# Layer 2 of a three stage kernel: one activation function, seven products of halves for y in four groups, and two sums kept in PSUM

## The chip, the cores and the metric

One core of a Trainium2 chip runs the whole program. The metric is the device time of one execution in microseconds. A kernel is timed several times and the median is given. Beside that, one execution is recorded by the profiler; all rows in this document come from such an execution, and their times count from the start of its span.

## The reference

Three stages follow each other: a linear attention over 4 x 8 heads, whose output is a matrix x of 2304 tokens by 512, and then two dense layers that both widen 512 to 2048 and narrow again.

```python
def _moe_ref(x, w_in, w_out):             # layer 1
    h = x @ w_in
    g = h - np.tanh(h)
    return (g @ w_out).astype(np.float32)

def _moe2_ref(x, w_in, w_out):            # layer 2
    h = x @ w_in
    g = h * (1.0 / (1.0 + np.exp(-1.702 * h)))
    return (g @ w_out).astype(np.float32)
```

The change is in layer 2 and in the work that prepares it.

## The kernel before

**Arithmetic.** Every float32 operand of a dense product is held as two tiles, a rounded high half and the rest as a low half, and a product is three passes of TensorE (`PASSES`: high by high, high by low, low by high). The helper `two(hi, lo, src)` makes them: ScalarE copies `src` to the high half (L423), GpSimd subtracts it for the low half (L424). Weights arrive as 64 bit words and are converted on the way: `cast1` on ScalarE (L284, L286), `cast2a` and `cast2b` on VectorE (L290, L295).

**Layer 1** (`steps`) runs over blocks of 512 tokens; each step makes h for one slice of the 2048 (`h_mm`, L344, twelve matmuls), applies the activation on ScalarE, VectorE and GpSimd (`elem1`, L364 to L374), splits g (L356, L358) and, three steps later (`LAG`), adds the slice's part to y (`y_mm`, L382, twelve matmuls into the PSUM banks y0 to y3). At a block's end `evac` moves y out through VectorE (L403), and the next block's y can start only then.

**Preparing layer 2's weights.** They are needed as sums of quarter blocks, in high and low halves. `conv_ticks` makes them pair by pair (a pair is two slices of 128; `NPAIR` is 8): pieces 0 and 1 of a pair are w_in, pieces 2 and 3 are w_out. The work is cut into ticks "a", "b", "s", "c", "h", "d", "o", "e", which the loops of layer 1 (`L1_TICKS`, one group of ticks per step, pairs 0 to 2) and of layer 2 (`L2_TICKS`, pairs 3 to 7) emit between their own instructions. Pieces go to DRAM (`wfi`, `wfo`) and are loaded again when they are used. In layer 1 the pieces 1 and 3 share the tile `raw2`, and the split pieces wait in `stg` for their stores.

**Layer 2** runs over 24 groups (`GROUPS`): a group n is a pair j of slices for a superblock sb of 768 tokens, taken as 2 x 2 blocks of 384 tokens. Groups 0 to 15 alternate between superblocks 0 and 1; groups 16 to 23 are the third superblock, with pairs 7 down to 0. For h a group needs seven products of block sums instead of eight (`SLOTS`, names P1 to P7; `h_prod`, L813, six matmuls of 384 columns each), one in each of its seven slots. They gather in three PSUM banks a, b and c; `keep` copies a partial sum out (L866), `h_add` adds it to a later one (L862), which gives the four blocks G11, G12, G21 and G22 of h. The activation is a sigmoid on ScalarE (`sig`, L874) and a product on VectorE (`mul`, L877); `gsplit` makes the two halves (L883 on ScalarE, L884 on GpSimd). For y the group has eight chunks (`y_chunk`, L834, six matmuls of 384 columns each) into four PSUM banks `hs`, each added to `yacc` by VectorE (L844). The chunks of group n are emitted in the slots of group n + 1 and the first of n + 2 (`YS`).

**Order.** The program is scheduled by hand: each engine runs its instructions in the order in which the loop emits them. All loads and stores go through SyncE's queue; a store is kept in `later` and emitted at the next `flush`. x for a superblock is split in ticks (`xticks`), one per slot. SBUF pools are stacks: a pool opened in the place of a closed one waits, tile by tile, for the last user of what lay there. The pool `l2left` holds, in order of first use, `win`, `ssum`, `yacc`, `wout`, the seven x tiles of superblock 1, `sp`, `hx`, `sg`, `s7`, `s2` and the tiles of g; below it lay layer 1's x, its elementwise tiles with `ghi` and `glo`, and its late weights.

## Time and profile before

| | |
|---|---|
| Time, median of 3 runs | 918.24 us (916.91 to 918.79) |
| The profiled execution | 917.95 us, span 916.1 us |
| TensorE busy | 900.0 us, 98% of the span, 5192 matmuls |
| VectorE, ScalarE, GpSimd busy | 71%, 61%, 50% |
| Granted TensorE clock, mean | 0.998 of full speed |
| HBM read and written | 98.98 MB, 40.89 MB |

A row of the timeline gives the start in us, the time the instructions took, the engine, the line of the kernel, what was written from what, and how many instructions it merges; square brackets hold the idle time ahead of it and what ended it. PE is TensorE, PEld its weight loads, DVE VectorE, ACT ScalarE, POOL GpSimd, SP SyncE. Consecutive matmuls overlap, so the distance between two starts says more than a duration.

### The profile page before, as it was taken

How to read it: one execution, taken by the hardware profiler on the slowest of the kernel's cores; microseconds unless marked ns; L12 is line 12 of the kernel's file. 1: busy time of each engine (PE TensorE's matmuls, PEld its weight loads, DVE VectorE, ACT ScalarE, POOL GpSimd, SP SyncE). 2: the span in 40 equal slices, each digit the busy share in tenths (PEclk: the TensorE clock that was granted, in tenths of full speed). 3: DMA queues.
4: the chain of work that ended last, by engine and by line, in shares of the span. 5: the costliest groups of instructions: out<-in, count | busy, mean ns of one | idle time of the engine just before them, and what ended most of it. 6: DMA issues, size and time to landing. Idle time of an engine off the chain costs nothing.

```text
span 916.1 us, 14382 instructions
## 1 busy us (share of the span) xinstructions
PE 900.0 (98%) x5192; PEld 819.5 (89%) x5192; DVE 646.4 (71%) x1041; ACT 562.4 (61%) x1175; POOL 462.2 (50%) x361
## 2 busy tenths in 40 slices
PE   8999998999999999998999999999999999999998
PEld 6888887888889888887899889999999999999998
DVE  5899978756766665876867567588888888544454
ACT  5888878776777776767676644345555555433231
POOL 3555534556665665666766544244545564423222
PEclk9999999999999999999999999999999999999999
DMA  6788865131444421585572471224533211444532
GB/s 203 233 260 248 253 228 159 36 138 59 150 138 139 146 103 50 176 287 192 185 268 78 182 274 50 102 98 170 173 130 124 81 56 60 141 160 164 215 147 95
DMA packets 53224, 140.82 MB, mean 154 GB/s; under 512 B 6048, under 2 KB 12832, under 8 KB 50848
## 3 DMA queue, kind: packets, MB, share of 16 engines
q1 hardware_dynamic: 53008, 139.56, 45.0%
q8 instruction: 41, 0.67, 0.3%
q10 hardware_dynamic: 144, 0.33, 0.1%
q14 instruction: 31, 0.25, 0.1%
HBM read 98.98 MB, written 40.89 MB: 153 GB/s over the span
## 4 chain that ended last, share of the span: by engine, by line
PE 87%; DVE 4%; ACT 2%; DMA 2%; POOL 2%; issue 2%; ACTq 0%; POOLq 0%; DVEq 0%
PE hs L834 22%; PE y L382 19%; PE hs L344 18%; PE y L813 18%; PE y L201 3%; DMA raw<-w 2%; PE y L184 2%; PE y L125 1%; PE hs L153 1%; POOL mq L135 1%; DVE pq L139 1%; POOL stg L424 1%; PE hs L813 1%; PE y L228 1%; PE y L180 1%
## 5 line engine op out<-in xcount | busy, mean ns | idle before, releaser
L834 PE MATMUL hs<-g,wout 128*128 128x384 f32 x1152 | 225.4, 334 | 0.0
L344 PE MATMUL hs<-xb,w 128*128 128x512 f32 (+1 forms) x960 | 211.1, 370 | 1.5 <-DVE t L373 1.5
L834 PEld LDWEIGHTS hs<-g,wout 128*128 128x128 f32 x1152 | 202.0, 188 | 0.1
L344 PEld LDWEIGHTS hs<-xb,w 128*128 128x128 f32 x960 | 168.6, 190 | 32.2 <-DVE t L373 1.7
L382 PE MATMUL y<-ghi,w 128*128 128x512 f32 (+1 forms) x640 | 192.4, 368 | 3.2 <-DVE ye L403 3.2
L813 PE MATMUL y<-x,win 128*128 128x384 f32 x966 | 194.0, 335 | 1.3 <-DVE hx L862 1.2
L884 POOL TENSOR_TENSOR g<-sg,g 128x384 fp32r<-128x384 f32 x96 | 103.1, 1074 | 164.7 <-ACT g L883 164.5
L813 PEld LDWEIGHTS y<-x,win 128*128 128x128 f32 x966 | 169.4, 188 | 3.4 <-DVE hx L862 3.4
L358 POOL TENSOR_TENSOR glo<-wq,ghi 128x512 fp32r<-128x512 f32 x72 | 98.2, 1363 | 137.3 <-ACT ghi L356 137.3
L374 DVE COPY_PREDICATED wq<-m,t 128x512 f32<-128x512 uint16 x72 | 83.1, 1155 | 107.4 <-POOL wq L372 107.2
L844 DVE TENSOR_TENSOR yacc<-hs,yacc 128x384 f32<-128x384 f32 x168 | 92.1, 553 | 82.1 <-PE hs L834 81.7
L382 PEld LDWEIGHTS y<-ghi,w 128*128 128x128 f32 x640 | 116.6, 189 | 23.7 <-ACT ghi L356 3.6
L382 PE MATMUL y<-glo,w 128*128 128x512 f32 (+1 forms) x320 | 117.8, 368 | 0.0
L883 ACT CAST g<-sg 128x384 fp32r<-128x384 f32 x96 | 49.5, 515 | 93.8 <-DVE sg L877 93.8
L372 POOL TENSOR_TENSOR wq<-wq,s 128x512 f32<-128x512 f32 x70 | 90.5, 1293 | 20.0 <-DVE wq L371 20.0
L874 ACT ACTIVATE sg<-hx 128x384 f32<-128x384 f32 x72 | 37.9, 526 | 98.8 <-DVE hx L862 97.6
L135 POOL PARTITION_ALL_REDUCE mq<-pq x32 | 65.9, 2107 | 61.5 <-ACT pq L133 61.5
L364 ACT ACTIVATE s<-hs 128x512 f32<-128x512 f32 x72 | 42.9, 596 | 59.6 <-PE hs L344 59.5
L382 PEld LDWEIGHTS y<-glo,w 128*128 128x128 f32 x320 | 60.3, 189 | 9.9
L295 DVE SCALAR_TENSOR_TENSOR raw<-raw 128x512 int32<-128x512 int32 x57 | 61.8, 1084 | 1.6
L371 DVE SCALAR_TENSOR_TENSOR wq<-wq,hs 128x512 f32<-128x512 f32 x72 | 49.0, 681 | 15.7 <-ACT t L366 15.7
L356 ACT CAST ghi<-wq 128x512 fp32r<-128x512 f32 x72 | 44.2, 614 | 22.5 <-DVE wq L374 22.5
(116 smaller groups left out, 1285.4 us busy)
## 6 DMA issues: line engine op xcount, KB each, us to landing
raw<-w SPq DMA_DIRECT2D x57, 512.0 KB, 4.6
xb<-xs SPq DMA_DIRECT2D x24, 512.0 KB, 6.2
win<-wfi SPq DMA_DIRECT2D x9, 1280.0 KB, 8.4
wout<-wfo SPq DMA_DIRECT2D x9, 1024.0 KB, 4.8
vt<-v SPq DMA_DIRECT2D x16, 325.0 KB, 3.5
kt<-kT SPq DMA_DIRECT2D x15, 320.0 KB, 3.4
qt<-qT SPq DMA_DIRECT2D x16, 288.0 KB, 3.5
wfi<-stg SPq DMA_DIRECT2D x9, 512.0 KB, 4.2
```

Source lines behind the costliest of these rows:

```text
L135: nc.gpsimd.partition_all_reduce(mqs[i, j], pq[:, j, :], channels=128, reduce_op=bass.bass_isa.ReduceOp.max)
L295: nc.vector.scalar_tensor_tensor(out=c, in0=c, scalar=3, in1=z, op0=ALU.logical_shift_left, op1=ALU.bitwise_or)
L344: nc.tensor.matmul(h[:, j * n:j * n + n], w[:, 0, a, kt * 128:kt * 128 + 128], x[:, c, kt, :n], start=(k == 0), stop=(k == 11))
L358: nc.gpsimd.tensor_tensor(out=lo, in0=g, in1=hi.bitcast(F32), op=ALU.subtract)
L372: (nc.vector if si < 2 else nc.gpsimd).tensor_tensor(out=w, in0=w, in1=s, op=ALU.mult)
L374: nc.vector.copy_predicated(out=w, mask=m.bitcast(mybir.dt.uint16), data=t)
L382: nc.tensor.matmul(y[d][:, :n], w[:, 1, a, d * 128:d * 128 + 128], g[c][:, j * n:j * n + n], start=(first and j == 0 and k == 0), stop=(la ...
L813: nc.tensor.matmul(dst, w[:, WID[name], a, kt * 128:kt * 128 + 128], xt[:, kt, c, :], start=(first and k == 0), stop=(k == 5), skip_group_ ...
L834: nc.tensor.matmul(dst, wout[j][:, f, a, d * 128:d * 128 + 128], gt[n, f, t][:, c, :], start=(k == 0), stop=(k == 5))
L844: nc.vector.tensor_tensor(out=u, in0=dst, in1=u, op=ALU.add)
L883: nc.scalar.copy(out=u[:, 0, :], in_=g)
L884: nc.gpsimd.tensor_tensor(out=u[:, 1, :], in0=g, in1=u[:, 0, :].bitcast(F32), op=ALU.subtract)
```

## The change

- The activation becomes one ScalarE function (`Gelu_apprx_sigmoid`); `mul` goes. The preload of the table before layer 2 is changed with it.
- `h_add` for G11 (from group 1 on) and for G21 writes its sum back into a PSUM bank, where the activation reads it; `hx` has two tiles.
- In groups 17 to 20 y is formed from seven products of halves (`y_prod`, `y_add`) in place of eight chunks. They need four differences of g blocks (`forms`, `tform`, `tsplit`) on GpSimd, with splits of their own, and four sums of w_out blocks. A product fills two banks, so the four `hs` banks are closed for these groups and opened again after them.
- The sums of w_out for the pairs 3 to 6 are made in new ticks "f", "g" and "i" (`sums2`, `chs`), stored to `wfs`, and loaded by `load_wos`; the next pair's pieces 2 and 3 are loaded after those stores.
- Three low halves per pair go from GpSimd to VectorE in layer 2; in layer 1 `raw2` has two tiles, `stg` six, and the loads are issued earlier; the pool `x0` is opened after the preparation closes; the x tiles of superblock 1 get a pool of their own, `x1`, whose place `yb` takes from group 16 on; `load_win` goes ahead of `load_wout`; one x tick is moved by a slot.

```diff
+L2_STICKS = {2: "f", 3: "g", 6: "i"}
...
+YG, YE = 2 * NPAIR + 1, 3 * NPAIR - NPRE
+YP = ("P3", "P1", "P2", "P6", "P7", "P5", "P4")
...
+    hbanks, banks = ExitStack(), ExitStack()
...
+    psh = pool("psumh", hbanks, space=bass.MemoryType.PSUM)
...
+    wfs = dp.tile([NPAIR, 128, 4 * 512], F32, name="wfs")
...
     def pt(tag):
-        return ps.tile([128, 512], F32, tag=tag, name=tag, bufs=4 if tag == "hs" else 1)
+        return (psh if tag == "hs" else ps).tile([128, 512], F32, tag=tag, name=tag, bufs=4 if tag == "hs" else 1)
...
-            nc.scalar.activation(out=ob, in_=qb, func=AF.Sigmoid)
+            nc.scalar.activation(out=ob, in_=qb, func=AF.Gelu_apprx_sigmoid)
...
-    def two(hi, lo, src, eng=None):
+    def two(hi, lo, src, eng):
...
-        (eng or nc.gpsimd).tensor_tensor(out=lo, in0=src, in1=hi.bitcast(F32), op=ALU.subtract)
+        eng.tensor_tensor(out=lo, in0=src, in1=hi.bitcast(F32), op=ALU.subtract)
...
         def load(q, k):
...
-                t = raw[q, k] = o.tile([128, 512, 2], I32, tag=tag, name="raw2", bufs=1 if tag == "raw2" else 2)
+                t = raw[q, k] = o.tile([128, 512, 2], I32, tag=tag, name="raw2", bufs=2)
...
+        def sums2(q):
+            s = st[q] = p.tile([128, 4, 256], F32, tag="ssum", name="ssum", bufs=1)
+            f1, f2 = f32(q, 2), f32(q, 3)
+            a11, a21, a12, a22 = f1[:, :256], f1[:, 256:], f2[:, :256], f2[:, 256:]
+            for o, x, y, op in (
+                    (s[:, 0, :], a21, a22, ALU.add), (s[:, 2, :], a11, a21, ALU.subtract),
+                    (s[:, 1, :], s[:, 0, :], a11, ALU.subtract), (s[:, 3, :], a12, s[:, 1, :], ALU.subtract)):
+                nc.gpsimd.tensor_tensor(out=o, in0=x, in1=y, op=op)
+        def chs(q, i):
+            t = raw[q, 2 + i // 2].rearrange("p a b -> p (a b)").bitcast(F32R)
+            v = t.rearrange("p (a h c) -> p a h c", h=2, c=256)
+            two(v[:, :, 0, :], v[:, :, 1, :], st[q][:, i:i + 2, :], nc.gpsimd)
+            store(wfs[q, :, i * 512:(i + 2) * 512].rearrange("p (a h c) -> p a h c", h=2, c=256), v.bitcast(F32))
+            later.append((now[0], lambda: load(q + 1, 2 + i // 2)))
         def ch(q, src, i, n):
...
-                t = p.tile([128, 2 * 512], F32R, tag="stg", name="stg", bufs=3)[:, :512 * n]
+                t = p.tile([128, 2 * 512], F32R, tag="stg", name="stg", bufs=6)[:, :512 * n]
...
-            two(v[:, :, 0, :], v[:, :, 1, :], src.rearrange("p (a c) -> p a c", c=256))
+            two(v[:, :, 0, :], v[:, :, 1, :], src.rearrange("p (a c) -> p a c", c=256),
+                nc.vector if place and i == 2 else nc.gpsimd)
...
-                v = p.tile([128, 2 * 512], F32R, tag="stg", name="stg", bufs=3)
+                v = p.tile([128, 2 * 512], F32R, tag="stg", name="stg", bufs=6)
...
-            two(v[:, 0, :], v[:, 1, :], f32(q, k))
+            two(v[:, 0, :], v[:, 1, :], f32(q, k), nc.vector if place else nc.gpsimd)
...
             def last22():
...
-                load(*((q + 1, 1) if place else (q, 3)))
+                load(q + 1, 1)
...
             def out(k):
...
-                load(q + 1, k if place or k == 2 else 1)
+                if not place or q == NPAIR - 1:
+                    load(q + 1, k)
...
         def begin():
-            for k in range(4 if place else 3):
+            for k in range(4):
...
-        return begin, [(x, f) for q in pairs for x, f in pieces(q).items()]
+        extra = [(x, f) for q in pairs if q < NPAIR - 1 for x, f in dict(
+            f=lambda q=q: sums2(q), g=lambda q=q: chs(q, 0), i=lambda q=q: chs(q, 2)).items()]
+        return begin, [(x, f) for q in pairs for x, f in pieces(q).items()], extra
...
-    ticks, xticks = deque(), deque()
+    ticks, sticks, xticks = deque(), deque(), deque()
...
-            xpool[0] = pool("x0", side="right", reuse_waits="tile")
-            for i in range(7):
-                new_x2(0, i)
...
-            begin, ts = conv_ticks(rp, range(NPRE))
+            begin, ts, _ = conv_ticks(rp, range(NPRE))
...
-                for x in L1_TICKS[(sp - LAG - 1) % len(L1_TICKS)]:
+                at = sp - LAG - 1
+                for x in L1_TICKS[at % len(L1_TICKS)]:
...
+                xpool[0] = pool("x0", side="right", reuse_waits="tile")
+                for i in range(7):
+                    new_x2(0, i)
...
+    wos = {}
+    def load_wos(j):
+        wos[j] = yb.tile([128, 4, 2, 256], F32R, tag="wos", name="wos", bufs=2)
+        nc.sync.dma_start(
+            out=wos[j].bitcast(F32), in_=wfs[j].rearrange("p (a h c) -> p a h c", h=2, c=256))
+    ybank, begun = {}, set()
+    def y_prod(n, name):
+        sb, j = GROUPS[n]
+        i = "c" if name in ("P2", "P7", "P4") else "a"
+        if name in ("P1", "P2", "P7"):
+            ybank[n, i] = psb.tile([128, 2, 512], F32, tag="ya" if (i == "a") == (n % 2 == 0) else "yc", name="yb", bufs=1)
+        dst = ybank[n, i]
+        w = dict(P1=lambda a: wout[j][:, 0, a, :256], P2=lambda a: wout[j][:, 1, a, :256],
+                 P4=lambda a: wout[j][:, 1, a, 256:], P5=lambda a: wos[j][:, 0, a], P6=lambda a: wos[j][:, 1, a],
+                 P7=lambda a: wos[j][:, 2, a], P3=lambda a: wos[j][:, 3, a])[name]
+        g = gf[n, dict(P1="B11", P2="B21", P3="B22", P4="T4", P5="T1", P6="T2", P7="T3")[name]]
+        for d in range(2):
+            for k, (a, c) in enumerate(PASSES):
+                nc.tensor.matmul(
+                    dst[:, d, :TW], w(a)[:, d * 128:d * 128 + 128], g[:, c, :],
+                    start=(name in ("P1", "P2", "P7") and k == 0), stop=(k == 2), skip_group_check=True)
+    def y_add(n, name):
+        sb, j = GROUPS[n]
+        src = ybank[n, "c" if name in ("P2", "P7", "P4") else "a"][:, :, :TW]
+        h, t = dict(P1=(0, 0), P2=(0, 0), P3=(0, 1), P4=(1, 0), P5=(1, 1), P6=(1, 0), P7=(1, 1))[name]
+        u = yacc[sb, t, h]
+        nc.vector.tensor_tensor(out=u, in0=src, in1=u, op=ALU.add)
...
-    def h_add(n, i, x, y):
-        t = hx[n, i] = tt("hx", 3)
+    def h_add(n, i, x, y, t=None):
+        t = hx[n, i] = tt("hx", 2) if t is None else t
...
-    def sig(n, i):
-        t = sg[n, i] = tt("sg", 4)
-        nc.scalar.activation(out=t, in_=hx[n, i], func=AF.Sigmoid, scale=1.702)
-    def mul(n, i):
-        nc.vector.tensor_tensor(out=sg[n, i], in0=hx.pop((n, i)), in1=sg[n, i], op=ALU.mult)
+    def act(n, i):
+        if yform(n) and i in (G21, G12):
+            t = sg[n, i] = yb.tile([128, TW], F32, tag="sgb", name="sgb", bufs=3)
+        else:
+            t = sg[n, i] = tt("sg", 4)
+        nc.scalar.activation(out=t, in_=hx.pop((n, i)), func=AF.Gelu_apprx_sigmoid)
+    gf = {}
...
     def gsplit(n, i):
...
-        u = gt[n, f, t] = l2.tile([128, 2, TW], F32R, tag=f"g{f}{t}", name=f"g{f}{t}", bufs=1 if f != t else 2)
-        g = sg.pop((n, i))
+        u = l2.tile([128, 2, TW], F32R, tag=f"g{f}{t}", name=f"g{f}{t}", bufs=1 if f != t else 2)
+        if not yform(n):
+            gt[n, f, t] = u
+        else:
+            gf[n, f"B{f + 1}{t + 1}"] = u
+        g = sg[n, i]
...
+    def tform(n, i, x, y):
+        t = sg[n, i] = yb.tile([128, TW], F32, tag=i, name=i, bufs=1)
+        nc.gpsimd.tensor_tensor(out=t, in0=sg[n, x], in1=sg[n, y], op=ALU.subtract)
+    def tsplit(n, i):
+        u = gf[n, i] = yb.tile([128, 2, TW], F32R, tag=f"f{i}", name=f"f{i}", bufs=1)
+        nc.scalar.copy(out=u[:, 0, :], in_=sg[n, i])
+        nc.gpsimd.tensor_tensor(out=u[:, 1, :], in0=sg[n, i], in1=u[:, 0, :].bitcast(F32), op=ALU.subtract)
...
+    def forms(n, s):
+        if s == 0:
+            tform(n, "T1", G12, G11)
+        elif s == 1:
+            tform(n, "T2", G22, "T1")
+            tsplit(n, "T2")
+        elif s == 2:
+            tform(n, "T3", G22, G12)
+            tsplit(n, "T3")
+        elif s == 3:
+            tsplit(n, "T1")
+        elif s == 4:
+            tform(n, "T4", G21, "T2")
+            tsplit(n, "T4")
+        elif s == 5:
+            gsplit(n, G22)
+    def yform(n):
+        return YG <= n < YE
...
     def vec(n, s):
...
-                h_add(n, G11, a, sv.pop((n, "sp")))
-            if n:
-                mul(n - 1, G12)
+                h_add(n, G11, a, sv.pop((n, "sp")), bank[n, "b"][:, :TW] if n else None)
+            if n and not yform(n - 1):
...
-                sig(n, G11)
+                act(n, G11)
...
-            if n:
+            if n and not yform(n - 1):
...
-                mul(n, G11)
...
-                h_add(n, G21, c, sv.pop((n, "s2")))
+                h_add(n, G21, c, sv.pop((n, "s2")), c)
...
-                sig(n, G21)
+                act(n, G21)
...
-                mul(n, G21)
-                sig(n, G22)
+                act(n, G22)
...
-                mul(n, G22)
...
-                sig(n, G12)
+                act(n, G12)
+        if yform(n - 1):
+            forms(n - 1, s)
...
-    l2 = wpool[1] = xpool[1] = pool("l2left", reuse_waits="tile")
+    l2 = wpool[1] = pool("l2left", reuse_waits="tile")
+    x1 = ExitStack()
+    xpool[1] = pool("x1", x1, reuse_waits="tile")
...
+            if n == 2 * NPAIR and s == 0:
+                x1.close()
+                yb = pool("yb", reuse_waits="tile")
...
-                if n >= m:
+                if n >= m and not yform(n - m):
...
+            m = n - 1 if s else n - 2
+            if m == YG and s == 1:
+                hbanks.close()
+                psb = pool("psumb", banks, space=bass.MemoryType.PSUM, reuse_waits="tile")
+            if yform(m):
+                y_prod(m, YP[s])
...
+            if yform(m):
+                y_add(m, YP[s])
+                if m == YE - 1 and s == 0:
+                    banks.close()
+                    psh = pool("psumh2", space=bass.MemoryType.PSUM, reuse_waits="tile")
...
+            if s == 0 and n > 2:
+                if n == 3:
+                    load_win(2)
+                elif sb == 0 and j < NPAIR - 1:
+                    new_w(j + 1)
+                elif sb == 2 and 0 < j < NPAIR - 1:
+                    load_win(j - 1)
...
-            if s == 0 and n > 2:
-                if n == 3:
-                    load_win(2)
-                elif sb == 0 and j < NPAIR - 1:
-                    new_w(j + 1)
-                elif sb == 2 and 0 < j < NPAIR - 1:
-                    load_win(j - 1)
+            if s == 0 and yform(n):
+                load_wos(j)
...
-                if 3 <= q < 98 or q > 100:
+                if 3 <= q < 98 and q != 6 or q > 100:
...
-                begin, ts = conv_ticks(l2, range(NPRE, NPAIR), place)
+                begin, ts, ss = conv_ticks(l2, range(NPRE, NPAIR), place)
...
-            if ticks:
-                at = q - 7 * (2 * NPRE - 2)
+                sticks.extend(ss)
+            at = q - 7 * (2 * NPRE - 2)
+            if ticks and at >= 0:
...
-                    if at >= 0 and ticks[0][0] == x:
+                    if ticks[0][0] == x:
...
+            if sticks and at >= 14 and at // 7 % 2 == 0 and s in L2_STICKS:
+                assert sticks[0][0] == L2_STICKS[s]
+                sticks.popleft()[1]()
...
-                assert not ticks
+                assert not ticks and not sticks
```

## Rows read from the trace of the kernel before

**Rows 1.** busy time by stretch: length, then busy us of each engine, clock, DMA

```profile
420.00:440.00 20.00, 16.80 (x75) 13.62 (x74) 14.16 (x20) 13.05 (x23) 12.54 (x10) 1.00 0.64 213
440.00:540.00 100.00, 100.00 (x539) 87.48 (x538) 63.39 (x87) 63.23 (x114) 59.35 (x48) 1.00 0.52 183
...
560.00:900.00 340.00, 340.00 (x1956) 338.52 (x1955) 234.77 (x404) 153.64 (x325) 141.74 (x127) 1.00 0.34 124
```

**Rows 2.** timeline at 430 us: start, us, engine, line, tiles, idle before

```profile
429.00 2.88 PE L344 MATMUL hs<-xb,w 128*128 128x512 f32 x12
...
430.67 0.67 ACT L284 ACTIVATE raw<-raw 128x512 f32<-128x512 f32 x1 [2.91 <-DMA raw<-w]
...
432.63 1.70 DVE L295 SCALAR_TENSOR_TENSOR raw<-raw 128x512 int32<-128x512 int32 x1
...
434.26 2.47 DVE L403 TENSOR_TENSOR ye<-y,ye 128x512 f32<-128x512 f32 x4
...
435.08 0.47 PE L382 MATMUL y<-ghi,w 128*128 128x512 f32 x1 [3.20 <-DVE ye L403]
```

**Rows 3.** chain of waits in the same stretch: start, us, what

```profile
420.12 3.08 POOL stg L424 x2
423.22 7.43 DMA raw<-w
```

**Rows 4.** DMA issues: tiles, queue, count, size, us to landing

```profile
raw<-w SPq DMA_DIRECT2D x57, 512.0 KB, 4.6
...
wfi<-win SPq DMA_DIRECT2D x9, 512.0 KB, 2.6
...
wfo<-wout SPq DMA_DIRECT2D x6, 512.0 KB, 6.0
```

**Rows 5.** timeline of TensorE in the third block

```profile
841.40 1.20 PE L813 MATMUL y<-x,win 128*128 128x384 f32 x6
...
842.44 1.20 PE L834 MATMUL hs<-g,wout 128*128 128x384 f32 x6
```

**Rows 6.** lines by shape: count, busy us, mean ns, idle before

```profile
L844 DVE TENSOR_TENSOR yacc<-hs,yacc 128x384 f32<-128x384 f32 x168 | 92.1, 553 | 82.1 <-PE hs L834 81.7
...
L883 ACT CAST g<-sg 128x384 fp32r<-128x384 f32 x96 | 49.5, 515 | 93.8 <-DVE sg L877 93.8
L373 DVE TENSOR_TENSOR t<-hs,t 128x512 f32<-128x512 f32 x72 | 49.1, 682 | 0.0
...
L877 DVE TENSOR_TENSOR sg<-hx,sg 128x384 f32<-128x384 f32 x72 | 47.8, 664 | 0.0
...
L874 ACT ACTIVATE sg<-hx 128x384 f32<-128x384 f32 x72 | 37.9, 526 | 98.8 <-DVE hx L862 97.6 <-POOL x L424 1.2
...
L424 POOL TENSOR_TENSOR win<-raw,win 128x256 fp32r<-128x256 f32 x5 | 3.7, 744 | 4.7 <-ACT win L423 4.7
```

**Rows 7.** timeline of GpSimd and VectorE in the third block

```profile
833.89 1.01 POOL L884 TENSOR_TENSOR g<-sg,g 128x384 fp32r<-128x384 f32 x1 [2.30 <-ACT g L883]
834.32 0.56 DVE L844 TENSOR_TENSOR yacc<-hs,yacc 128x384 f32<-128x384 f32 x1 [1.06 <-PE hs L834]
```

**Rows 8.** the same two engines in the blocks before it

```profile
670.10 1.47 POOL L884 TENSOR_TENSOR g<-sg,g 128x384 fp32r<-128x384 f32 x1
...
671.08 0.90 DVE L877 TENSOR_TENSOR sg<-hx,sg 128x384 f32<-128x384 f32 x1
```

**Rows 9.** timeline at the start of layer 2

```profile
537.76 3.31 PE L813 MATMUL hs<-x,win 128*128 128x384 f32 x18
...
544.87 1.37 DVE L877 TENSOR_TENSOR sg<-hx,sg 128x384 f32<-128x384 f32 x1
...
547.09 0.55 DVE L862 TENSOR_TENSOR hx<-y,sp 128x384 f32<-128x384 f32 x1
...
547.69 1.34 PE L813 MATMUL y<-x,win 128*128 128x384 f32 x6 [1.20 <-DVE hx L862]
```

**Rows 10.** lines by shape, the table load ahead of layer 2

```profile
L370 ACT ACT_TABLE_LOAD x1 | 1.3, 1283 | 0.0
```

## The prediction

> **What bounds the kernel now.** I read the busy time by stretches first. From 440 to 540 us and from 560 to 900 us TensorE is busy all the time; from 420 to 440 us it lacks 3.2 us [rows 1], and another 1.2 us near 547 us. So two things shorten the span: fewer matmuls, or a closed hole. What an edit saves on another engine beside a full TensorE is worth nothing, and what it adds there costs nothing until TensorE waits for it.
>
> **The hole at 432 us.** It is one wait of 3.20 us, for VectorE's evacuation of y (L403). The evacuation begins at 434.26 us, behind L295 of a weight conversion; that conversion began with ScalarE's L284, which had waited 2.91 us for a raw load [rows 2]. The chain of waits goes on from there: the load, 7.43 us, was issued when GpSimd had split the pieces of the pair before [rows 3]. The cause is in the buffers: layer 1's `raw2` is one tile, so piece 1 of the next pair is loaded only after `out(3)` has split piece 3, little more than a step before its use.
>
> **Part 1, layer 1's buffers (`raw2` two tiles, `stg` six, `x0` opened later).** Piece 1 is now loaded in tick "ch" of the pair before, four steps ahead of its use. A step is twelve matmuls of h and twelve of y, each twelve at most 2.88 us [rows 2], so some 22 us for a load of 7.4 us. The wait goes, ScalarE is level with TensorE, and L403 can start when the last y ends at 429.0 us; its first piece is wanted at 431.9 us. I take the whole 3.2 us. The other bound is 0: VectorE's own queue, where L295 takes 1.70 us [rows 2], keeps L403 late. `x0` over the preparation's tiles costs nothing: its first tile over a staging tile is written two steps after the last stores are issued, and the stores of this size land in 2.6 to 6.0 us [rows 4].
>
> **Part 2, seven products in four groups (17 to 20).** A group has 48 y matmuls of 384 columns, after the change 7 x 2 x 3 = 42. Six matmuls take 1.04 us (841.40 to 842.44 us) [rows 5], 0.1733 us each. With its 42 of h a group goes from 90 x 0.1733 = 15.60 to 84 x 0.1733 = 14.56 us: 24 matmuls and 4.16 us less in all. What has to hide under it:
>
> VectorE: seven adds of 768 elements from PSUM for eight of 384. None is in the trace; from 553 ns at 384 and 682 ns at 512 elements [rows 6] the slope gives 0.94 us, two old adds 1.11 us at most. With three sums for h at the 384 price: 8.2 to 9.4 us. A product's bank is wanted again two slots (4.16 us) later, so nobody waits.
>
> ScalarE: seven casts of 515, four activations of 526 ns [rows 6] and three copies of at most that: 7.3 us.
>
> GpSimd is the tight one: four differences and seven low halves. In this block one takes 1.01 us, also where VectorE's add from PSUM runs beside it [rows 7]. Three times the low half follows its difference at once and waits for ScalarE's cast, with 0.07 us either side 0.66 us. Sum 11 x 1.01 + 3 x 0.66 = 13.1 us. By slots of 2.08 us from the group's start: T2's cast stands behind the copy `s7`, which needs P7 of h, and ends at about 4.3 us; then come the low half of T2, T3, its low half, those of G11 and T1, T4, its low half: 4.4 + 7 x 1.01 + 2 x 0.66 = 12.8 us. P4 wants the last in slot 6 behind six matmuls of h, 13.5 us. Slack 0.7 us; the other products have over 1. No wait while an operation stays under 1.11 us. The upper end of its price is 1.47 us, a low half beside VectorE's product of two SBUF tiles [rows 8].
>
> On these two rows the Trainium skill (SBUF — State Buffer, Who interferes with whom) has a rule: GpSimd shares VectorE's second port, so VectorE instructions with two SBUF inputs contend with its reads, those with one do not. By it this block, where VectorE keeps only sums with a PSUM input, saves its 4.16 us; by the dearer row alone it would be the first rival below. The moved low halves of part 4 contend by it, beside a TensorE that does not wait for them.
>
> Loads: 1 MB more per group on SyncE (`wos`), last in the queue, wanted 21 us after its issue; half of it lands in 4.6 us [rows 4]. `win` now goes ahead of `wout`. Nothing.
>
> **Part 3, one function for the activation.** It takes 96 products from VectorE (72 of them 47.8 us) [rows 6] and adds nothing on ScalarE. The function has no row; I take the sigmoid's 526 ns, bounds 515 (a cast) and twice it. The sums put back into PSUM I take at the 553 ns of an add into SBUF, bounds that and the 682 ns of a longer one. Beside a full TensorE none of it counts, except at 547 us. There P6 of group 1 waits 1.20 us for the sum hx of 547.09 us, behind L877 with 1.37 us and pieces of the x preparation [rows 9]. That product goes, and the tick of slot 6, with two VectorE pieces, is skipped: the sum comes some 2 us earlier, and the 1.2 us go.
>
> Against it: with `x1` in its own pool, `sp`, `hx` and `sg` move down over the last `ghi` and `glo` tiles. By the tile sizes, the first `sg` lies over the low half that the last `do_y` reads, until TensorE goes on to h at 537.76 us [rows 9]. The first activation then ends near 538.5 us, copy `s7` behind it at 539.0, just where P4 wants it: 0.1 to 0.2 us. Net 1.0 us gained. Bounds: 1.4 gained; 1.2 lost, if `hx` too has to wait for that `do_y`.
>
> **Part 4, side work of groups 4 to 13.** Per pair GpSimd gets four sums (a 256 wide low half takes 0.74 us) [rows 6] and two low halves of 512 and hands three to VectorE; VectorE gets those, at 0.7 to 1.7 us, and loses eight products of 0.66 us. Neither becomes fuller by much. Two stores of 512 KB are added, and the next pair's pieces 2 and 3 are loaded only after them. Piece 2: low half done some 11 us into the even group, store 2.6 to 6.0, load 4.6 us [rows 4], so 18 to 22 us, wanted at about 19 us. ScalarE may wait up to 3 us at tick "c" in four pairs; the cast of G11 and the activation of G21 stand behind it, and TensorE needs their results over 4 us later. I take nothing; the other end is half of it, four times: 6 us.
>
> **Sum.** The profiled execution took 917.95 us (span 916.1), 0.3 below the median of 918.24. 917.95 - 3.2 - 4.16 - 1.0 = 909.6; 909.8 halfway to the median's basis.
>
> **The rivals.**
> GpSimd becomes the bound of the four groups (the other side). For: 13.1 of 14.56 us and 0.7 us of slack. Against: 1.01 us in this block. At 1.47 us a group takes 11 x 1.47 + 2.0 = 18.2 us, 3.6 over 14.56: 909.8 + 14.5 = 924. The whole turns into a loss from 1.33 us per operation. 5%.
> The hole at 432 us stays, since VectorE's queue sets it and not the load: 913.0. For: L295 at 1.70 us. Against: all of that queue hangs behind the load. 11%.
> Layer 2 starts later by the new places of its tiles: 911 to 912. 11%.
> Pieces 2 and 3 come late and TensorE follows: up to 915.8. 8%.
> The function's table lacks the scaled copy of the conversions (L284, L286), and ScalarE loads two tables per conversion, 1.28 us each [rows 10]: 20 conversions, 51 us on an engine that is 61% busy, above 930. Against: the sigmoid brought one load. The Trainium skill (ScalarE: Activation LUTs, Table sets: the hidden batching unit) says that copy is in every set. 2%.
>
> **How the numbers follow.** The forecast as summed has 63%; its own range is 908.3 to 911. With the hole that stays and the late start, 85% lie within 908.2 to 914.2. A difference under 0.2% (1.8 us) can hardly be told from none: faster than that has 0.89, within it 0.05 (late pieces, or GpSimd near 1.33 us), slower 0.06.
>
> **What would show it.** 5168 matmuls; no wait of y L382 near 430 us and no waits of L284 for raw loads in layer 1; four groups of 14.56 us from about 807 us on with a full TensorE and GpSimd operations of 1.01 us; no hole at 547 us, the first activation of layer 2 near 538 us. Wrong: TensorE waiting for a low half in those groups, low halves above 1.11 us there, a third table load, or waits of L284 after 600 us that TensorE follows.

## Result and the profile after

After the change the median is 909.00 us (908.53 to 909.25, 4 runs) against 917.58 (916.65 to 918.79, 4 runs) before: a ratio of 0.9905, 95% interval 0.9888 to 0.9922. The forecast was 909.8 us. The profiled execution took 908.87 us (span 907.1) against 917.95 (916.1) before: 9.1 us, of which the prediction's three terms are 8.36. TensorE has 5168 matmuls and is busy 895.0 us (900.0 before), VectorE 621.7 us (69%), ScalarE 568.3 (63%), GpSimd 500.5 (55%). HBM moves 4.2 MB more in each direction.

By stretches of the profile after (length, then busy us of TensorE, weight loads, VectorE, ScalarE, GpSimd; clock, DMA) TensorE is full where [rows 1] lacked 3.2 us, and in the stretches of layer 2's start and of the four groups:

```profile
420.00:440.00 20.00, 19.96 (x89) 16.25 (x88) 14.98 (x23) 15.10 (x28) 12.62 (x10) 1.00 0.76 249
...
540.00:560.00 20.00, 20.00 (x118) 20.00 (x117) 15.42 (x24) 11.20 (x27) 13.77 (x12) 1.00 0.44 156
...
807.00:866.00 59.00, 59.00 (x342) 59.00 (x341) 33.73 (x42) 25.98 (x58) 42.88 (x44) 1.00 0.66 256
```

The timeline after, at the end of the block and at the start of layer 2:

```profile
428.74 2.88 PE L351 MATMUL hs<-xb,w 128*128 128x512 f32 x12
...
430.83 2.48 DVE L410 TENSOR_TENSOR ye<-y,ye 128x512 f32<-128x512 f32 x4
...
431.66 0.47 PE L389 MATMUL y<-ghi,w 128*128 128x512 f32 x1
...
534.34 3.34 PE L841 MATMUL hs<-x,win 128*128 128x384 f32 x18
534.36 0.53 ACT L937 ACTIVATE sg<-hx 128x384 f32<-128x384 f32 x1 [3.11 <-PE y L389]
...
540.98 0.57 DVE L922 TENSOR_TENSOR y<-y,sp 128x384 f32<-128x384 f32 x1 [0.76 <-PE y L841]
...
541.75 1.20 PE L862 MATMUL hs<-g,wout 128*128 128x384 f32 x6
...
542.79 1.20 PE L841 MATMUL y<-x,win 128*128 128x384 f32 x6
```

**The hole at 432 us** is closed: the evacuation of y (L403 before, L410 now) starts 2.1 us behind the first of the twelve matmuls of h, not 5.3 us [rows 2], and the first y starts 0.2 us later than in a full stream (2.92 us behind that first matmul, where twelve take 2.72). **The start of layer 2:** the sum that P6 of group 1 waited 1.20 us for [rows 9] begins 1.8 us ahead of P6 now, where it began 0.6 us ahead, and the two groups of six start 1.04 us apart: no wait there. The first activation waits for the last `do_y`, as the prediction's places said, and ends at 534.89 us; no TensorE instruction waits behind it. Counted from start to start, TensorE's lead over the trace of before is 0.26 us ahead of the hole at 432 us (it has this by 147 us, ahead of the stretches that the prediction named), 3.42 us behind it, 5.04 us behind the start of layer 2, 4.82 us ahead of the four groups and 9.0 us at the end. So 3.16 us come from the closed hole, 1.62 us from layer 2's start and 4.2 us from the four groups, and 0.2 us are lost between 560 and 800 us.

In a group of seven products, T4, its cast, its low half and P4, which wants that half, by the same timeline:

```profile
829.76 1.01 POOL L954 TENSOR_TENSOR T<-sgb,T 128x384 f32<-128x384 f32 x1
...
830.80 0.52 ACT L958 CAST fT<-T 128x384 fp32r<-128x384 f32 x1 [2.22 <-POOL T L954]
...
831.39 1.01 POOL L959 TENSOR_TENSOR fT<-T,fT 128x384 fp32r<-128x384 f32 x1 [0.62 <-ACT fT L958]
...
833.46 1.20 PE L902 MATMUL yb<-fT,wout 128*128 128x384 f32 x6
```

This is group 18: the low half ends at 832.40 us, 1.05 us before P4 (0.7 predicted). Groups 19 and 20 have the same slack; in group 17, the first of the four, it is 0.57 us (818.33 and 818.90 us). The new operations, lines by shape (count, busy us, mean ns, idle before), of the four groups first and then the activation over the whole span:

```profile
L911 DVE TENSOR_TENSOR yacc<-yb,yacc 128x768 f32<-128x768 f32 x28 | 26.8, 957 | 23.1 <-PE yb L902 23.1
L959 POOL TENSOR_TENSOR fT<-T,fT 128x384 fp32r<-128x384 f32 x16 | 16.3, 1017 | 13.9 <-ACT fT L958 13.9
...
L937 ACT ACTIVATE sg<-y 128x384 f32<-128x384 f32 x61 | 30.1, 493 | 112.5 <-DVE y L922 107.4 <-PE y L841 5.2
L937 ACT ACTIVATE sg<-hx 128x384 f32<-128x384 f32 x25 | 13.1, 525 | 28.2 <-DVE hx L922 24.0 <-PE y L389 3.1 <-POOL x L431 1.2
```

The sum of 768 elements takes 0.96 us (0.94 predicted), the function 525 ns from SBUF (the sigmoid's 526 was taken) and 493 ns from PSUM. One table load stands ahead of layer 2, as before [rows 10].

### The profile page after: what moved, and what is told of

Read it like the earlier page. It is cut to its first block, busy times and chain, and to the rows that moved or that the text cites. A ratio compares the mean times of both kernels' runs of the same rounds, so it can differ in the third digit from the quotient of the medians.

```text
span 907.1 us, 14395 instructions
## 1 busy us (share of the span) xinstructions
PE 895.0 (99%) x5168; PEld 815.2 (90%) x5168; DVE 621.7 (69%) x956; ACT 568.3 (63%) x1195; POOL 500.5 (55%) x398
## 4 chain that ended last, share of the span: by engine, by line
PE 87%; DVE 8%; issue 2%; ACT 2%; POOL 1%; ACTq 0%; POOLq 0%; DVEq 0%
PE y L389 22%; PE hs L351 21%; PE y L841 15%; PE hs L862 15%; PE yb L902 3%; PE y L208 3%; PE y L191 2%; PE y L132 1%; DVE yacc L872 1%; PE hs L160 1%; DVE raw L302 1%; POOL mq L142 1%; DVE ssum L459 1%; PE hs L841 1%; DVE pq L146 1%
## 5 line engine op out<-in xcount | busy, mean ns | idle before, releaser
L862 PE MATMUL hs<-g,wout 128*128 128x384 f32 x960 | 187.5, 334 | 0.0
L365 POOL TENSOR_TENSOR glo<-wq,ghi 128x512 fp32r<-128x512 f32 x72 | 100.4, 1394 | 138.5 <-ACT ghi L363 138.5
L862 PEld LDWEIGHTS hs<-g,wout 128*128 128x128 f32 x960 | 168.3, 188 | 0.0
L381 DVE COPY_PREDICATED wq<-m,t 128x512 f32<-128x512 uint16 x72 | 88.5, 1230 | 104.9 <-POOL wq L379 103.8
L950 POOL TENSOR_TENSOR g<-sg,g 128x384 fp32r<-128x384 f32 x88 | 100.2, 1144 | 83.0 <-ACT g L949 69.5
L872 DVE TENSOR_TENSOR yacc<-hs,yacc 128x384 f32<-128x384 f32 x136 | 74.0, 552 | 68.4 <-PE hs L862 68.2
L937 ACT ACTIVATE sg<-y 128x384 f32<-128x384 f32 x61 | 30.1, 493 | 112.5 <-DVE y L922 107.4
L371 ACT ACTIVATE s<-hs 128x512 f32<-128x512 f32 x72 | 42.9, 596 | 64.0 <-PE hs L351 63.9
L302 DVE SCALAR_TENSOR_TENSOR raw<-raw 128x512 int32<-128x512 int32 x57 | 57.7, 1012 | 1.7
L372 ACT ACTIVATE wq<-s,qb 128x512 f32<-128x512 f32 x72 | 52.3, 726 | 7.3 <-POOL glo L365 1.0
```

The lines of the kernel that those rows point to most:

```text
L302: nc.vector.scalar_tensor_tensor(out=c, in0=c, scalar=3, in1=z, op0=ALU.logical_shift_left, op1=ALU.bitwise_or)
L365: nc.gpsimd.tensor_tensor(out=lo, in0=g, in1=hi.bitcast(F32), op=ALU.subtract)
L372: nc.scalar.activation(out=w, in_=s, func=AF.Square, scale=QS, bias=qb)
L381: nc.vector.copy_predicated(out=w, mask=m.bitcast(mybir.dt.uint16), data=t)
L862: nc.tensor.matmul(dst, wout[j][:, f, a, d * 128:d * 128 + 128], gt[n, f, t][:, c, :], start=(k == 0), stop=(k == 5))
L872: nc.vector.tensor_tensor(out=u, in0=dst, in1=u, op=ALU.add)
```

## Experiments

Each kernel's own runs are compared with the 909.0 us of after or, for parts put into the kernel before, with runs of before on the same chip; a ratio is always against those runs of before. Their medians lie between 916.9 and 918.9 us from one experiment to the next, so differences of a microsecond from after are read from the traces, not from the times.

**Layer 1's buffers alone**, in the kernel before:

```diff
-    ... bufs=1 if tag == "raw2" else 2)
+    ... bufs=2)
-                load(*((q + 1, 1) if place else (q, 3)))
+                load(q + 1, 1)
-                load(q + 1, k if place or k == 2 else 1)
+                load(q + 1, k)
-            for k in range(4 if place else 3):
+            for k in range(4):
```

> The kernel before with two raw2 tiles and the earlier loads of pieces 1 and 3, and nothing else of the change (stg stays at three tiles, x0 where it was). If the late raw load makes the hole at 432 us, the wait of y L382 there falls from 3.20 us to under 0.3 us and the time by 3.0 to 3.4 us. If VectorE's own queue or the staging tiles make it, the wait stays above 1.5 us and the time falls by less than 1.7 us.

914.0 us (912.3 to 914.79, 6 runs) against 916.92: ratio 0.9959 [0.9944, 0.9974], 2.9 us. Its timeline, 2.4 us ahead of that of before when it comes to the block's end:

```profile
426.56 2.88 PE L344 MATMUL hs<-xb,w 128*128 128x512 f32 x12
429.46 0.47 PE L382 MATMUL y<-ghi,w 128*128 128x512 f32 x1
...
542.07 1.33 PE L813 MATMUL y<-x,win 128*128 128x384 f32 x6 [1.20 <-DVE hx L862]
```

The y that waited 3.20 us now starts 2.90 us behind the twelve matmuls of h, as in after; from start to start the lead over before grows by 3.19 us here, and from 150 us on nowhere else, while the 1.20 us of layer 2 stay. The hole was the late load, and the two waits are separate.

**Chunks kept.** After, with eight chunks in all groups; the sums of w_out are still made and stored.

```diff
 def yform(n):
-    return YG <= n < YE
+    return False
...
```

> The changed kernel with all y in chunks: groups 17 to 20 keep eight chunks, no forms, no load of wos (its sums are still made and stored). If the 24 matmuls are the whole worth of this part, the time is that of the changed kernel plus 4.16 us, 913.2 us, and 5192 matmuls run. If the side work of groups 4 to 13 or the seven products cost TensorE something, the difference is another: above 4.5 or under 3.8 us.

913.29 us (910.73 to 913.75, 6 runs), 4.3 over after: the 24 matmuls are worth what the starts said. Both kernels do the side work of groups 4 to 13, so this difference doesn't hold its price; the waits further below do.

**The function alone**, in the kernel before, with the product gone:

```diff
-        nc.scalar.activation(out=t, in_=hx[n, i], func=AF.Sigmoid, scale=1.702)
+        nc.scalar.activation(out=t, in_=hx.pop((n, i)), func=AF.Gelu_apprx_sigmoid)
...
-        nc.vector.tensor_tensor(out=sg[n, i], in0=hx.pop((n, i)), in1=sg[n, i], op=ALU.mult)
+        pass
```

> The kernel before with the one function and without the product, and nothing else of the change. If the product in front of the sum hx makes the hole at 547 us, 0.9 to 1.5 us are gained and the wait of y L813 there falls under 0.4 us. If the skipped tick of the x preparation is what closes it, the wait stays above 0.7 us and less than 0.6 us is gained. Either way nothing is gained later in layer 2.

914.87 us (913.51 to 918.95, 12 runs), ratio 0.9978 [0.9963, 0.9993]: 0.6 to 3.4 us, the middle 2.0. The timeline (the third row is two matmuls behind the hole):

```profile
434.22 0.47 PE L382 MATMUL y<-ghi,w 128*128 128x512 f32 x1 [2.16 <-DVE ye L403]
...
434.76 1.04 PE L382 MATMUL y<-ghi,w 128*128 128x512 f32 x2
...
547.61 1.34 PE L813 MATMUL y<-x,win 128*128 128x384 f32 x6 [0.27 <-DVE hx L862]
```

The product's 1.37 us ahead of the sum [rows 9] were most of the wait of 1.20 us; 0.27 stay. The gain's middle lies above the 0.9 us that the wait became shorter, and the trace shows where more came from: something is gained later in layer 2, against the expectation. Between 560 and 800 us TensorE counts as busy all the time in before [rows 1], yet its weight loads wait five times for a sum (L862) that stands behind a product. The first line is the wait (total, times, longest), the other the product ahead of the first such sum, which starts at 625.38 us:

```profile
PEld y L813 <- DVE hx L862: 1.5, 5, 0.3
...
624.09 0.90 DVE L877 TENSOR_TENSOR sg<-hx,sg 128x384 f32<-128x384 f32 x1
```

With the function alone no weight load waits there, and the lead over before grows by 1.35 us from start to start. The hole at the block's end is 2.16 us in this execution and 3.20 us in that of before, though this kernel changes nothing in layer 1's steps or loads; so it seems to differ between executions, which two traces don't show.

**GpSimd's slack.** After, with one or two GpSimd subtractions more per group ahead of T3; the results are not used.

```diff
+            for _ in range(2):        # one in the second kernel
+                dummy(n)
             tform(n, "T3", G22, G12)
```

> The changed kernel with two more GpSimd subtractions of 384 elements in each of the groups 17 to 20, ahead of T3; their results are not used. If GpSimd is close to the bound as worked out (1.0 us of slack at P4 in the trace after, 2.0 us more work per group), TensorE waits about 1 us for the low half of T4 in each group and the time rises by 3 to 5 us against the changed kernel. If GpSimd's slack is larger than that, the time rises by less than 0.8 us.

> After, with one GpSimd subtraction more (1.01 us) in each of groups 17 to 20, ahead of T3; its result is not used. The trace of after shows T4's low half ending 1.05 us before P4 is wanted, so one more operation just fits: 909.0 to 909.5 us. With the 0.7 us of slack worked out beforehand it would be 0.3 us too much four times: 910.2 us. If GpSimd's whole queue counted and not this chain, 11 more would fit nowhere else either, and the time would rise by the full 1.01 us four times: 913 us.

Two: 913.08 us (912.37 to 914.31, 5 runs), 4.1 over after. One: 909.49 us (908.76 to 910.33, 4 runs), 0.5 over after with ranges that overlap. The waits of the weight loads in the four groups (total, times, longest), with two:

```profile
PEld yb L902 <- POOL fT L959: 4.1, 8, 0.9
```

and with one:

```profile
PEld yb L902 <- POOL fT L959: 0.4, 1, 0.4
```

By the slacks of 0.57 us in group 17 and 1.05 us in the other three, two more should cost some 1.45 + 3 x 0.97 = 4.4 us, and one some 0.4 us, all of it in group 17. Counted from start to start TensorE loses 4.0 us in the four groups with two and 0.4 us with one, there alone. What decides is this chain's slack, not GpSimd's busy share (42.9 of 59 us).

**What makes GpSimd dear.** After, with VectorE subtractions behind each sum of y in groups 17 to 20; the results are not used. First two of SBUF tiles, then one, then one with a PSUM operand (the edit in short; `zz` is a tile of zeros in SBUF):

```diff
 y_add(m, YP[s])
+for _ in range(2):                   # two SBUF tiles; twice, then once
+    nc.vector.tensor_tensor(out=t, in0=zz, in1=zz, op=ALU.subtract)
...
+nc.vector.tensor_tensor(out=t, in0=bank, in1=zz, op=ALU.subtract)   # the bank just added
```

> The changed kernel with two VectorE subtractions of a zero tile in SBUF after each y sum of the groups 17 to 20, so that VectorE has two SBUF inputs beside GpSimd; their results are not used. If such instructions hold GpSimd up, its operations there rise from 1.01 us to 1.2 us or more, the low half of T4 comes later than P4 wants it, and the time rises by 2 us or more against the changed kernel (up to 14 us at 1.47 us each). If they do not, GpSimd stays at 1.01 us and the time rises by less than 0.8 us, since VectorE has about 4 us free in a group.

> After, with one VectorE subtraction of two SBUF tiles of 128x384 behind each of the seven sums of y in groups 17 to 20; the result is not used. VectorE goes to some 8.3 + 7 x 0.6 to 0.8 = 12.5 to 14 us of a group's 14.56, so it is not full. If such an operation takes GpSimd's reads away, GpSimd's operations beside it go from 1.01 to 1.3 or 1.4 us, the low half of T4 comes 1 to 2 us later against 1.05 us of slack, and the time is 909.5 to 912 us. Rival: only VectorE's fullness cost time in the run with twice as many; then nothing is lost here, 909.0 to 909.3 us, and GpSimd stays at 1.01 us.

> The same seven VectorE subtractions per group with one operand in PSUM (the bank just added) in place of SBUF; the result is not used. If only two SBUF operands take GpSimd's reads away, GpSimd stays at 1.01 us, VectorE takes 8.3 + 7 x 0.56 = 12.2 us of 14.56, and the time is that of after, 909.0 to 909.5 us. Rival: any VectorE operation beside GpSimd slows it; then GpSimd and the time are as with two SBUF operands.

Two per sum: 923.06 us (922.86 to 923.28, 4 runs), 14.1 over after. That is near the 924 us of the prediction's rival, but not for its reason alone. VectorE is full there (53 subtractions of 812 ns beside 8 us of sums per group), and TensorE's waits in these groups name VectorE:

```profile
PE yb L902 <- DVE yacc L911: 3.1, 4, 0.9
PE y L841 <- DVE y L922: 2.9, 4, 0.9
PE y L841 <- DVE hx L922: 2.3, 4, 0.6
```

This run doesn't separate the two causes; the other two do. One of SBUF tiles: 910.13 us (908.64 to 910.27); one with PSUM: 909.56 us (908.45 to 909.85), 4 runs each. The difference in time is inside the ranges, but the traces are plain. With SBUF tiles weight loads wait three times for a low half, 0.5 us in all; with PSUM none waits in the four groups. The lines by shape, with SBUF tiles:

```profile
L965 DVE TENSOR_TENSOR dummy<-zz 128x384 f32<-128x384 f32 x27 | 21.1, 780 | 0.0
...
L954 POOL TENSOR_TENSOR T<-sg,sgb 128x384 f32<-128x384 f32 x4 | 5.5, 1368 | 0.0
```

and with a PSUM operand:

```profile
L965 DVE TENSOR_TENSOR dummy<-yb,zz 128x384 f32<-128x384 f32 x27 | 14.8, 548 | 0.0
...
L954 POOL TENSOR_TENSOR T<-sg,sgb 128x384 f32<-128x384 f32 x4 | 4.1, 1015 | 0.0
```

The timeline with SBUF tiles shows how it comes about:

```profile
825.75 0.55 DVE L965 TENSOR_TENSOR dummy<-zz 128x384 f32<-128x384 f32 x1
825.81 1.36 POOL L954 TENSOR_TENSOR T<-sg,sgb 128x384 f32<-128x384 f32 x1
...
827.80 1.02 POOL L959 TENSOR_TENSOR fT<-T,fT 128x384 fp32r<-128x384 f32 x1 [0.63 <-ACT fT L958]
827.83 1.40 DVE L965 TENSOR_TENSOR dummy<-zz 128x384 f32<-128x384 f32 x1
```

Whichever starts first runs at its own pace, 0.55 or 1.02 us, and the other is longer by most of what is left of it (0.35 of 0.49 us, 0.85 of 0.99 us): the pair isn't slowed alike. The Trainium skill (SBUF — State Buffer, SBUF: two separate sides) describes this as an exclusive lock that the first holds for its whole instruction while the other is blocked; these rows agree in the order, and fall 0.14 us short of a full block both times.

**More groups.** After, with a fifth group (21): pair 2's sums are made in layer 1, in the two steps behind its last tick, at the last of which SyncE issues their stores and then the loads of x. A sixth group (22) takes pair 1 as well, with its sums between the ticks.

```diff
-YG, YE = 2 * NPAIR + 1, 3 * NPAIR - NPRE
+YG, YE = 2 * NPAIR + 1, 3 * NPAIR - NPRE + 1     # + 2 for six groups
...
+            ticks.extend(ss)
...
-                for x in L1_TICKS[at % len(L1_TICKS)]:
+                for x in L1_TICKS[at % 6] if at < 18 else ("f", "gi", "")[at - 18 if at < 20 else 2]:
```

> The changed kernel with seven products in group 21 as well; the w_out sums of pair 2 are made in two steps of layer 1 that had no tick. If matmuls alone count, six fewer save 1.04 us: 0.9989 of the changed kernel, 908.0 us. If the three ticks more in layer 1 or the store ahead of the x preparation hold TensorE up, it is not faster than the changed kernel.

> The same with group 22 too; the sums of pair 1 are made in ticks of pair 2 in layer 1, and pieces 2 and 3 of pair 2 are loaded after them. If matmuls alone count, 2.08 us less than the changed kernel, 906.9 us. If the later loads hold ScalarE up as in the kernel before, a hole of 1 to 3 us comes back in layer 1 near 430 us or at the next block's end, and the gain is eaten up.

Five: 918.81 us (917.15 to 919.86, 12 runs), ratio to before 1.0015 [1.0005, 1.0026]. Six: 923.65 us (922.51 to 924.75, 6 runs), ratio 1.0069 [1.0052, 1.0085], with two waits, of 6.2 and 5.2 us. With five, from the chain of waits (start, us, what):

```profile
464.02 2.98 POOL raw L431 x2
...
467.01 0.32 SPq L427
...
469.21 7.16 DMA xi<-ysf
```

TensorE's timeline, and then the stretches around it:

```profile
484.50 0.55 PE L389 MATMUL y<-ghi,w 128*128 128x256 f32 x1 [8.88 <-DVE ye L410]
```

```profile
480.00:490.00 10.00, 5.50 (x25) 5.53 (x26) 7.36 (x11) 5.92 (x12) 6.25 (x6) 0.50 0.43 158
490.00:500.00 10.00, 10.00 (x62) 8.97 (x62) 7.88 (x12) 6.14 (x12) 6.17 (x5) 0.98 0.18 52
```

The stores wait in SyncE's queue for GpSimd's low halves, the loads of x are issued behind them, and ScalarE and VectorE wait for those loads with layer 1's own work queued behind: a hole of 8.88 us where 1.04 was to be gained.

So the sums were put a step earlier, and the conversion of x a step later and in another rhythm; then the four sums and one low half were given to VectorE as well.

```diff
+                for x in {17: "oef", 18: "gi"}.get(at, L1_TICKS[at % 6] if at < 17 else ""):
...
-            elif sp > XSTEP and xticks:
-                for _ in range(1 + (sp - XSTEP) % 5 % 2):
+            elif sp > XSTEP + 1 and xticks:
+                for _ in range(1 + (sp - XSTEP - 1) % 2):
...
-                nc.gpsimd.tensor_tensor(out=o, in0=x, in1=y, op=op)     # second kernel only
+                (nc.gpsimd if place else nc.vector).tensor_tensor(out=o, in0=x, in1=y, op=op)
```

> Five groups of seven products, with the sums of the fifth one step of layer 1 earlier than in the run that lost, so that the low halves are done before the stores are issued, and the conversion of x one step later. If the 8.9 us hole there came from SyncE's queue standing behind these low halves alone, it is gone: 6 matmuls less than with four groups, 1.04 us, so 908.0 us (907.5 to 908.7), 5162 matmuls, TensorE full from 460 to 500 us. Rival: the added work in the last steps of layer 1 is too much for GpSimd or VectorE wherever it stands: a hole of 2 to 6 us stays between 460 and 490 us and the time is 910 to 915 us.

> The version with five groups and the sums of the fifth one step earlier, with those four sums and the second of the two low halves on VectorE. In the version with all of them on GpSimd that queue was full from 456 to 467 us (two low halves of 3.06 us, four sums of 3.2, two low halves of 3.01, beside 2.6 us of layer 1's own work per step of 5.5), layer 1's activation fell behind, and the evacuation of y at the block's end came 2.7 us late, in all some 5.6 us over 908.0. If GpSimd's queue is the cause, it now has 5.7 us in a step of 5.5 and 4.1 in the next, VectorE 5.6 and 4 to 5, and TensorE stays full: 908.0 us (907.5 to 909). Rival: VectorE's operations on two SBUF tiles beside GpSimd stretch both, and the step is late as before: 910 to 914 us.

Earlier: 913.64 us (913.06 to 914.26, 4 runs). On VectorE: 912.32 us (909.49 to 916.8, 10 runs). Neither reaches after. In the first, the hole shrinks but stays, at the same place (the other waits in the last steps are 0.80 us and less):

```profile
480.36 0.36 PE L389 MATMUL y<-ghi,w 128*128 128x256 f32 x1 [2.67 <-DVE ye L410]
```

and in the second GpSimd is relieved, but two of VectorE's sums of SBUF tiles run beside its low halves and take 1.5 us where the other two take 0.4. Further down, three pieces of the conversion of x stand right ahead of the evacuation:

```profile
454.01 1.52 DVE L468 TENSOR_TENSOR ssum<-raw,raw 128x256 f32<-128x256 f32 x1
455.45 1.51 DVE L468 TENSOR_TENSOR ssum<-raw 128x256 f32<-128x256 f32 x1
456.88 0.41 DVE L468 TENSOR_TENSOR ssum<-ssum,raw 128x256 f32<-128x256 f32 x1
...
474.58 0.55 DVE L558 TENSOR_TENSOR xi<-xi 128x384 f32<-128x384 f32 x1
...
475.51 1.63 DVE L558 TENSOR_TENSOR xi<-xi 128x384 f32<-128x384 f32 x1
477.06 2.47 DVE L410 TENSOR_TENSOR ye<-y,ye 128x512 f32<-128x512 f32 x4
...
477.89 0.36 PE L389 MATMUL y<-ghi,w 128*128 128x256 f32 x1 [2.33 <-DVE ye L410]
```

SyncE's queue was thus only part of it. The rest isn't separated: the three pieces take 2.5 us from the first start to that of L410, in both versions, where in after one piece stands there (0.5 us). By these rows some 2.0 us of the holes of 2.67 and 2.33 us come from the new rhythm of the conversion and not from the sums. Neither the sums in these steps with the old rhythm nor sums two or three steps earlier were tried, so whether layer 1's last steps have room for another pair stays open. No version here beats after.

## Why the prediction was right

**Layer 1's buffers, 3.2 us:** right in cause and size. After lost the wait, and the buffers alone bring 2.9 us. Counted from start to start the hole was 435.08 - 431.72 = 3.36 us, of which 0.20 us stay in after: 3.16 us.

**Seven products, 4.16 us:** 4.2 us in the trace, 4.3 us by the run without them. The working for GpSimd held: 1.01 us per operation, T4's low half 12.5 us into the group, 12.95 in group 17 (12.8 predicted), a slack of 1.05 us, 0.57 in group 17 (0.7 predicted).

**The start of layer 2, 1.0 us net:** the term that was mis-sized; it measured 1.62. Two things. The wait was priced by its idle time, 1.20 us; but consecutive matmuls overlap, and the six of L834 ahead of it started at 545.20 us, so P6 was due at 546.24 and started at 547.69 [rows 9], 1.45 us late; the next six followed after 1.18 us, not 1.04. And the 0.1 to 0.2 us subtracted for the new places of `sg` were not lost: the activation waited 3.11 us exactly where the prediction put it, but nothing on TensorE waited for it. With starts for idle times the three terms are 3.16 + 1.59 + 4.16 = 8.9 us, and the trace gives 9.0.

**The stretch from 560 to 800 us, taken as nothing:** here the sum came out by luck. The prediction read this stretch as full, priced the lost products at nothing beside it (part 3) and the side work of groups 4 to 13 too (part 4). Neither is nothing. Without the products the five waits of the weight loads go, 1.35 us by the run with the function alone; in after four waits stand in the same places, behind a low half of w_out that part 4 moved to VectorE, ahead of the sum:

```profile
PEld y L841 <- DVE y L922: 1.6, 4, 0.4
...
619.03 1.04 DVE L431 TENSOR_TENSOR wout<-raw,wout 128x512 fp32r<-128x512 f32 x1
...
621.06 1.31 PE L841 MATMUL y<-x,win 128*128 128x384 f32 x6
```

The two all but cancel: 0.2 us are lost. Whether those waits go when that low half stays on GpSimd was not tried.

**The rivals.** GpSimd did not become the bound; one operation of 1.01 us more per group makes TensorE wait in group 17, two in all four. The hole did not stay. Layer 2 did not start later. Of late pieces 2 and 3 the trace shows nothing: ScalarE waits for no raw load, and its four waits for GpSimd's new sums (L468), up to 2.5 us, are not followed by TensorE. No table was loaded again. That this block keeps its price because VectorE has only sums with a PSUM input was put to the test by the subtractions above and held: GpSimd stayed at 1015 ns with a PSUM operand beside it and rose to 1368 with two SBUF tiles. The dearer price of 1.47 us [rows 8] was put down to the wrong instruction, though. The product L877 started 0.98 us behind that low half and was itself the longer one (0.90 us for 0.55); what ran beside the low half from its start, with two SBUF inputs, was the conversion:

```profile
668.96 1.74 DVE L295 SCALAR_TENSOR_TENSOR raw<-raw 128x512 int32<-128x512 int32 x1
```

## What to carry to other kernels

Price a wait of TensorE by the distance between starts or by the wait of its weight loads, not by the idle time in its row: a stretch in which it counts as busy throughout held 1.5 us of waits here. When work is added to an engine that is off the critical path, look for the one chain with the least slack and compare whole operations with that slack: here one more fits in three groups of four and two cost 4 us, at a busy share of 73%. Before VectorE work goes beside a tight GpSimd chain, see whether it reads two SBUF tiles: one operand in PSUM leaves GpSimd alone.

## What the hardware showed besides

A short hole can cost more than its length. Behind the wait of 2.16 us in the run with the function alone, two y matmuls take 1.04 us where those of the trace of before take 0.62, and the granted clock of 430 to 440 us is 0.83; from start to start the matmuls behind it lose another 1.6 us. With the 8.88 us of the fifth group's first version it is 0.50 from 480 to 490 us, the 1.2 GHz level, from within the hole to past its end at 484.50 us, and 0.98 after. In the profiled run of before, the hole of 3.20 us left the clock at 1.00, so this varies from run to run: of the 54 runs of before taken beside the experiments, the 22 with a mean granted clock of 0.998 have a median of 916.9 us, the 13 with 0.994 one of 919.0 us. All four runs of after have 0.998 and lie within 0.7 us. That the closed hole is what steadied them is borne out by counting: of the 66 runs of kernels that keep it (these of before, and the function alone) 18 have 0.994 or less, of the 37 of kernels that close it and make no other in layer 1 none, the six with the buffers alone (0.997 or more) among them. No run of before with 0.994 left a trace, so where its clock fell is not shown.
